# Value products of dilated local attention: the first halving as an accumulating DMA, longer VectorE steps, and h scaled when it is made

## The chip, the cores and the metric

The kernel runs on one NeuronCore of a Trainium2 chip. The metric is the device time of one execution in microseconds; less is better. The chip's engines run side by side, each in the order of its own instructions: TensorE (PE in the profile) does matrix products into eight PSUM banks, VectorE (DVE) does elementwise work on two operands, ScalarE (ACT) does copies and activations, GpSimd (POOL) here issues DMAs, and SyncE (SP) issues DMAs too.

## The reference

All inputs are bf16. `x` is 2048 x 1024.

```python
qkv = x @ wqkv                                   # 32 heads of 32; W, dil = 8, 2
idx = pos[:, None] - off[None, :]                # off = 0, 2, .. 14; masked where < 0
logits = einsum("bhsd,bhswd->bhsw", q, kg) * Dh ** -0.5     # kg = k[idx]
attn = softmax(where(mask, logits, -1e9))
a = einsum("bhsw,bhswd->bhsd", attn, vg) @ wo    # vg = v[idx]
b = (gelu(x @ w_gate) * (x @ w_up)) @ w_down     # Df = 3584
g = sigmoid((x * gate_w).sum(-1, keepdims=True))
return g * a + (1 - g) * b
```

So every position attends to itself and seven earlier positions at distances 2 to 14, in each head; a gated MLP runs beside it; a scalar gate per position mixes the two.

## The kernel before

**The products.** All large products go through a seven-product scheme (Strassen in Winograd's form): sums and differences of the blocks of both operands are made by VectorE, seven block products by TensorE, and their results are combined in PSUM by ScalarE's copies and VectorE's additions. The sequence is cut in two halves `s` of 1024 positions (`SUP`), these into chunks of 512 (`SC`). A `Unit` is one such product of the first stage: 28 matmuls of 128 x 512. There are 78 of them, in a written order: gate and up of pair 1 for half 0, 16 for q and k, 8 for v, then gate and up for the other pairs of hidden columns. There are `NPAIR` = 14 pairs; `NE_` = 12. In unit `b` TensorE runs p1 of `b`, p73 of `b - 1`, p5 and p26 of `b`, p4 of `b - 1`. Behind p73 stands VectorE's evacuation (L403), which reads the banks of two products that p4 and later steps write again.

**Background work.** All else on VectorE is done in tasks, Python generators that emit one step and yield its cost. At the end of each unit `run_bg` (L442) adds a period (4.7 before unit 26, then 4.8, and more where logit reductions take TensorE time) to a credit, keeping at most 0.3 of what was left, and takes steps of the first task in order of priority until the credit is at 0.3 or below. A step that yields None puts its task off to the next unit. So the order of VectorE's instructions is fixed when the kernel is written out, and depends on the costs that the tasks state.

- `h_task` (priority 0): `h_store` (L253) multiplies gelu(gate) by up for one pair and half (2048 elements a partition), and stores it to `h_d` by a DMA on GpSimd's queue. For the last two pairs it also multiplies by `omgrep`, which holds 1 - g.
- `sums_pair` (1): sums of the next pair's weights. `softmax` and `softmax_back` (1 and 3): one to three attention blocks of 256 positions (`AC`); the weights, times g, go to `attn_all` and from there to `w_d` in HBM.
- `qk_prods` (2): for one tile `t` of eight and one half, three products q by eight shifted k, 8 x 256 elements each, into `prod` tiles; TensorE sums them over the partitions of a head (`reduce_mm`). `spill` (4): the same for the fourth block of each half, where eight tiles are multiplied and added up on VectorE in two groups of four before the reduction.
- `t_forms`: sums of blocks of `w_down` and `wo`, stored in `t_d`.
- `pv_all` (4.2, then 5; L727): for each of eight blocks, in the order `PVO`, the attention weights come back from `w_d`, repeated over the partitions of a head, into `ab_`, and v from `v_d` into `vb`. For each of eight tiles one multiplication makes 2048 products (8 window positions by 256) in `prod2`, and for two tiles together the window is folded by three additions (L752), of 2048, 1024 and 512 elements:

```python
def mult(t):
    TT(out=prod2[(t // 2) % 2][:, t % 2], in0=ab, in1=_win_ap(v[:, t, HALO:HALO + AC], ...), op=ALU.mult)
def fold(t, w):
    ...
    TT(out=out_, in0=h(0), in1=h(1), op=ALU.add)      # w = 4, 2, 1
```

  A finished block goes from `ob_` to `o_d`.

**The down products.** From 512 us on, `down(0)` and `down(1)` multiply h and the attention output, as one matrix of 18 tiles (`NK`), by `w_down` and `wo`, for each half, in the seven-product scheme, and for most products once more inside (`level2`, matmuls of 128 x 256). Blocks A11 to A22 are loaded from `h_d` and `o_d`; where h was not scaled in `h_store`, `scale_task` (L913) multiplies it by `omgrep` after the load: for half 0 in the last units and at the start of `down(0)`, for half 1 within `down(1)`.

Of the kernel before, what the change touches and what calls it, by code (L numbers as in the profile page):

```python
# [9 lines left out]
ALU = mybir.AluOpType  # L10
# [5 lines left out]
P = 128  # L16
# [6 lines left out]
NJ = 4  # L23
# [45 lines left out]
def kernel(  # L69
# [54 lines left out]
    NE_ = NPAIR - 2  # L124
    h_d = [[tc.dram_tile([P, 4, k, SC], BF16, name=f"h_d{s}{e}") for e, k in enumerate((NE_, NPAIR - NE_))] for s in range(2)]
# [6 lines left out]
    w_d = tc.dram_tile([NBLK, 32, NJ, SC], BF16, name="w_d")  # L132
# [4 lines left out]
    with tc.manual_schedule(engines={mybir.EngineType.PE, mybir.EngineType.DVE, mybir.EngineType.Activation,  # L137
# [115 lines left out]
        def h_store(G, U, i, s):  # L253
            TT(out=flat(G), in0=flat(G), in1=flat(U), op=ALU.mult)  # L254
            if i >= NE_:
                om = omgrep[:, s * SUP:(s + 1) * SUP].rearrange("p (o s) -> p o s", o=1)
                TT(out=G, in0=G, in1=om.to_broadcast([P, 2, SUP]), op=ALU.mult)
            e = int(i >= NE_)
            i0 = 2 * (i - NE_ * e)
            nc.gpsimd.dma_start(out=h_d[s][e][:, :, i0 // 2, :], in_=flat(G).rearrange("p (hc s) -> p hc s", hc=4))  # L260
# [234 lines left out]
        def h_task(G, U, i, s):  # L495
            h_store(G, U, i, s)
            yield 1.14 if i < NE_ else 2.35
# [79 lines left out]
        pr_off = [R_PR + 4 * i for i in range(4)] + [R_PROD + 4 * i for i in range(2)]  # L577
# [3 lines left out]
        ab_ = [reg4(R_AB[i], NJ, NWIN, SJ) for i in range(2)]  # L581
        ob_ = [reg3(R_O[i], NT, AC) for i in range(2)]
        prod2 = [reg4(R_PROD2 + 8 * i, 2, NJ, NWIN * SJ) for i in range(2)]
# [16 lines left out]

        def reduce_mm(lg, src, start, stop):
            for j in range(NJ):
                nc.tensor.matmul(lg[32 * j:32 * j + 32, :], lhsT=R_[:], rhs=src[:, :, j * SJ:(j + 1) * SJ],
                                 start=start, stop=stop)
# [5 lines left out]
        def qk_prods(u, s, t):  # L610
            while reduced[0] < NT * s + t - t % 2:
                yield None
            out_ = []
            for a in range(ND):
                pr = prod_tile()
                qk_mult(pr, u.T[:, 0, a * AC:(a + 1) * AC], u.T[:, 1, a * AC:(a + 1) * AC])
                out_.append(pr)
                yield 1.14
            prods[t] = out_
            if t % 2:  # L620
                slotq.append(lambda: (qk_reduce(s, t - 1, prods[t - 1]), qk_reduce(s, t, out_)))
# [16 lines left out]

        def spill(s):
            while reduced[0] < 2 * NT:  # L640
                yield None
            accs = []
            temps = [prod_tile() for _ in range(2)]

            def mult(t, dst):
                qk_mult(dst, qb[s][:, t, :], kb[s][:, t, HALO:HALO + AC])

            def add(g, t):
                TT(out=accs[g], in0=accs[g], in1=temps[t % 2], op=ALU.add)

            for g in range(NT // QG):
                accs.append(prod_tile())
                mult(QG * g, accs[g])
                yield 1.14
                for t in range(1, QG):
                    mult(QG * g + t, temps[t % 2])
                    yield 1.14
                    if t > 1:
                        add(g, t - 1)
                        yield 1.14  # L660
                add(g, QG - 1)
                yield 1.2
            slotq.append(lambda: spill_reduce(s, accs))
# [36 lines left out]
        def softmax_back(a, cnt, ee, e4, sw, m, bc):  # L700
            while a // BPS not in gated:
                yield None
            d = m
            V.tensor_reduce(out=d, in_=sw, axis=AX.X, op=ALU.add)
            yield 0.9 * cnt + 0.05
            V.reciprocal(out=d, in_=d)
            TT(out=d, in0=d, in1=gblk[:, a:a + cnt, :], op=ALU.mult)
            yield 0.65 * cnt
            TT(out=attn_all[:, a:a + cnt, :].rearrange("p a (w s) -> p a w s", w=NWIN), in0=e4, in1=bc(d), op=ALU.mult)
            yield 0.55 * cnt + 0.05  # L710
            for j in range(NJ):
                nc.gpsimd.dma_start(out=w_d[a:a + cnt, :, j, :].rearrange("a h n -> h a n"),
                                    in_=attn_all[32 * j:32 * j + 32, a:a + cnt, :])
            ready.update(range(a, a + cnt))
            if a == 2 * BPS - 1:
                two[0] = True

        def pv_load(a, i):
            src = w_d[a].rearrange("h j n -> h (j n)")
            nc.sync.dma_start(out=ab_[i % 2].rearrange("p j w s -> p (j w s)"),  # L720
# [6 lines left out]
        def pv_all():  # L727
# [4 lines left out]
            yield None  # L732
            for i, a in enumerate(PVO):
# [8 lines left out]
                v, ab, o_ = vb[i % 2], ab_[i % 2], ob_[i % 2]  # L742

                def mult(t):
                    TT(out=prod2[(t // 2) % 2][:, t % 2], in0=ab,  # L745
                       in1=_win_ap(v[:, t, HALO:HALO + AC], [[SJ, NJ], [-DIL, NWIN], [1, SJ]]), op=ALU.mult)

                def fold(t, w):
                    pr = prod2[(t // 2) % 2]
                    h = lambda k: pr[:, :, :, k * w * SJ:(k + 1) * w * SJ]  # L750
                    out_ = h(0) if w > 1 else o_[:, t:t + 2, :].rearrange("p t (j s) -> p t j s", j=NJ)
                    TT(out=out_, in0=h(0), in1=h(1), op=ALU.add)  # L752

                mult(0)
                yield 1.14
                mult(1)
                yield 1.14
                for t in range(0, NT, 2):
                    if i + 1 == NBLK and t == 2:
                        load_A(Bs(0)["A12"], 0, 1, 0, 0, KX, False)  # L760
                    nxt = t + 2 < NT
                    if nxt:
                        mult(t + 2)
                        yield 1.14
                    fold(t, 4)
                    yield 1.14
                    if nxt:
                        mult(t + 3)
                        yield 1.14
                    fold(t, 2)  # L770
                    yield 0.68
                    fold(t, 1)
                    yield 0.4
                a0 = a % BPS % 2 * AC
                nc.gpsimd.dma_start(out=o_d[a // BPS][a % BPS // 2][:, :, a0:a0 + AC], in_=o_)
# [33 lines left out]
        pv_task = [bg(pv_all(), 4.2, QE + 3)]  # L809

# [53 lines left out]
        def t_forms():  # L864
            for q in range(NQ):
# [7 lines left out]
                for o_, a, b_ in ((r11, r12, r11), (r12, r22, r12), (r22, r22, r11), (r21, r21, r22)):  # L873
                    TT(out=flat(o_), in0=flat(a), in1=flat(b_), op=ALU.subtract)
                    yield 0.71
# [37 lines left out]
        def scale_task(b, s, c, ia, ib):  # L913
            t0 = s * SUP + c * SC
            om = omgrep[:, t0:t0 + SC].rearrange("p (o s) -> p o s", o=1)
            for i0 in range(ia, ib, 4):
# [153 lines left out]
        def down(s):  # L1070
# [112 lines left out]
            if not last:  # L1183
# [3 lines left out]
                take(rest, 3)  # L1187
# [120 lines left out]
```

## Time and profile before

| | |
|---|---|
| median of 3 runs | 720.22 us (719.84 to 720.38) |
| profiled execution | 720.06 us, span of its instructions 718.3 us |
| granted clock of TensorE | 1.000 |
| PE busy | 707.2 us |
| DVE busy | 673.2 us |
| ACT busy | 328.7 us |
| POOL busy | 134.5 us |
| DMA | 162.04 MB, mean 226 GB/s |

The span goes from the first instruction to the last; the execution's time has 1.8 us more around it. Busy time is the time in which an engine has an instruction running; instructions on PE and VectorE overlap a little, so that the sum of the durations is more than the busy time. A group's row has its line in the kernel, engine and operation, out<-in with the shapes, the count, then busy time and mean duration of one, then the engine's idle time just before and what ended it.

### The profile page before, as it was taken

The page shows a single profiled execution, that of the slowest core. Times are in us where ns is not written, and L with a number is a line of the kernel's source. Part 1 is how long each engine was busy: PE and PEld are TensorE (multiplying, and loading weights), DVE is VectorE, ACT ScalarE, POOL GpSimd, SP SyncE. Part 2 cuts the span into 40 slices and gives each one's busy share as a digit, 9 for nine tenths or more (in the row PEclk, how much of TensorE's full clock was granted, in tenths as well). Part 3 has the DMA queues.
Part 4 walks back from the last instruction along what each step waited for, and adds up shares of the span by engine and source line. Part 5 has one row for each costly group of instructions (what it writes and reads, how often), then busy time and mean ns, then how long its engine had stood idle before and what let it go on. Part 6 is the DMA issues. An engine that isn't in the chain of part 4 may idle for free. (4 is left out here: it accounts for less than half of the span.)

```text
span 718.3 us, 10752 instructions
## 1 busy us (share of the span) xinstructions
PE 707.2 (98%) x4051; PEld 408.2 (57%) x4107; DVE 673.2 (94%) x722; ACT 328.7 (46%) x600; POOL 134.5 (19%) x233
## 2 busy tenths in 40 slices
PE   8999999999999999999999999999999999999998
PEld 4466656655544444444444444444447886758887
DVE  2789989999999999999999999999999999899997
ACT  4554546444456665555555555555322321131431
POOL 1323544133210332121300000000210002110011
PEclk9999999999999999999999999999999999999999
DMA  9976643378264758574934836371891899995951
GB/s 276 284 183 219 229 142 122 106 247 304 102 205 127 231 197 252 175 221 149 294 115 152 280 123 214 124 288 59 300 427 52 307 401 396 420 429 223 379 213 60
DMA packets 92276, 162.04 MB, mean 226 GB/s; under 512 B 19280, under 2 KB 68848, under 8 KB 87872
## 3 DMA queue, kind: packets, MB, share of 16 engines
q1 hardware_dynamic: 75520, 105.46, 42.7%
q0 software_dynamic: 15984, 48.29, 19.3%
q10 hardware_dynamic: 720, 7.60, 2.7%
q8 instruction: 32, 0.52, 0.3%
q14 instruction: 20, 0.16, 0.1%
HBM read 112.17 MB, written 54.14 MB: 232 GB/s over the span
## 5 line engine op out<-in xcount | busy, mean ns | idle before, releaser
L366 PE MATMUL banks<-arena 128*128 128x512 bf16 x2136 | 472.1, 379 | 4.2 <-DVE arena L403 0.7
L366 PEld LDWEIGHTS <-arena 128*128 128x128 bf16 x2184 | 240.5, 111 | 235.3 <-issue 7.0
L1046 PE MATMUL banks<-arena 128*128 128x256 bf16 x1260 | 138.9, 273 | 0.8 <-DVE arena L1012 0.6
L1046 PEld LDWEIGHTS <-arena 128*128 128x128 bf16 x1260 | 123.1, 98 | 16.7 <-issue 1.5
L389 ACT COPY arena<-banks 128x512 f32<-128x512 f32 x78 | 45.8, 587 | 130.7 <-PE banks L366 130.7
L403 DVE TENSOR_TENSOR arena<-banks,arena 128x1024 bf16<-128x1024 f32 x78 | 95.2, 1221 | 11.0 <-PE banks L366 5.5
L374 ACT CAST arena<-banks 128x512 bf16<-128x512 f32 x102 | 59.7, 586 | 42.4 <-PE banks L366 42.4
L745 DVE TENSOR_TENSOR arena<-arena 128x2048 bf16<-128x2048 bf16 x64 | 77.0, 1220 | 0.5
L752 DVE TENSOR_TENSOR arena<-arena 128x2048 bf16<-128x2048 bf16 (+2 forms) x96 | 73.9, 776 | 1.0
L598 DVE TENSOR_TENSOR arena<-arena 128x2048 bf16<-128x2048 bf16 x64 | 74.7, 1219 | 0.1
L260 POOL DMA_DIRECT2D h_d<-arena x28 | 20.4, 730 | 226.5 <-DVE arena L254 195.4
L1079 PE MATMUL banks<-arena 128*128 128x512 bf16 x282 | 62.5, 379 | 0.3
L396 ACT COPY banks<-banks 128x512 f32<-128x512 f32 x78 | 44.5, 570 | 21.8 <-PE banks L366 20.0
L1004 DVE TENSOR_TENSOR arena<-arena 128x2304 bf16<-128x2304 bf16 x40 | 53.3, 1352 | 0.5
L384 ACT COPY banks<-banks 128x512 f32<-128x512 f32 x78 | 45.0, 576 | 13.6 <-PE banks L366 12.1
L1051 ACT COPY banks<-banks 128x256 f32<-128x256 f32 x60 | 21.4, 356 | 60.9 <-PE banks L1046 60.7
L1079 PEld LDWEIGHTS <-arena 128*128 128x128 bf16 x288 | 28.2, 98 | 33.5
L927 DVE TENSOR_TENSOR arena<-arena 128x2048 bf16<-128x2048 bf16 (+1 forms) x40 | 41.8, 1111 | 1.3 <-DMA arena<-h_d 1.3
L372 ACT ACTIVATE arena<-banks 128x512 bf16<-128x512 f32 x54 | 32.2, 597 | 15.4 <-PE banks L366 15.3
L323 DVE TENSOR_TENSOR arena<-arena 128x1024 bf16<-128x1024 bf16 x60 | 38.6, 685 | 0.5
L1012 DVE TENSOR_TENSOR arena<-arena 128x2304 bf16<-128x2304 bf16 x28 | 37.7, 1351 | 0.2
L254 DVE TENSOR_TENSOR arena<-arena 128x2048 bf16<-128x2048 bf16 x28 | 34.0, 1216 | 1.9 <-ACT arena L251 1.4
(93 smaller groups left out, 435.8 us busy)
## 6 DMA issues: line engine op xcount, KB each, us to landing
arena<-t_d SPq DMA_DIRECT2D x8, 2304.0 KB, 14.4
h_d<-arena POOLq DMA_DIRECT2D x28, 512.0 KB, 4.3
arena<-w_c SPq DMA_DIRECT2D x12, 1152.0 KB, 14.1
t_d<-arena POOLq DMA_DIRECT2D x36, 256.0 KB, 4.3
arena<-h_d SPq DMA_DIRECT2D x6, 1536.0 KB, 12.7
arena<-in_B_w_gate_dram SPq DMA_DIRECT2D x15, 512.0 KB, 5.7
arena<-in_B_w_up_dram SPq DMA_DIRECT2D x15, 512.0 KB, 5.3
arena<-in_B_w_down_dram SPq DMA_DIRECT2D x28, 256.0 KB, 6.6
```

Source lines behind the costliest of these rows:

```text
L366: self.pe = nc.tensor.matmul(ps, lhsT=self.L[form](kt), rhs=rhs[:, kt, :], start=(start and kt == 0), stop=(kt == HK - 1), skip_group_chec ...
L374: nc.scalar.copy(out=o_, in_=i_)
L384: nc.scalar.copy(out=self.Y, in_=self.X)
L389: nc.scalar.copy(out=self.p5s, in_=self.V)
L396: nc.scalar.copy(out=self.Z, in_=self.Y)
L403: TT(out=self.T[:, :, c2s], in0=pair, in1=self.p5s.rearrange("p (o n) -> p o n", o=1).to_broadcast([P, 2, SC]), op=ALU.add)
L598: TT(out=dst, in0=q.rearrange("p (o s) -> p o s", o=1).to_broadcast([P, NWIN, AC]), in1=_win_ap(k, [[-DIL, NWIN], [1, AC]]), op=ALU.mult)
L745: TT(out=prod2[(t // 2) % 2][:, t % 2], in0=ab, in1=_win_ap(v[:, t, HALO:HALO + AC], [[SJ, NJ], [-DIL, NWIN], [1, SJ]]), op=ALU.mult)
L752: TT(out=out_, in0=h(0), in1=h(1), op=ALU.add)
L1004: TT(out=o_, in0=a, in1=b_, op=op)
L1046: nc.tensor.matmul(c(i, h, j), lhsT=l[:, kt, j * P:(j + 1) * P], rhs=r[:, kt, :], start=False, stop=(kt == KH - 1), skip_group_check=True)
L1079: nc.tensor.matmul(ps, lhsT=L[:, i, j * P:(j + 1) * P], rhs=R[:, i, :], start=(start and q == 0), stop=(q == NK - 1), skip_group_check=not ...
```

## The change

- **Value products.** `mult` makes one tile, or two in one instruction of 4096 elements where the credit is above 1.5. The addition that folds eight window positions to four is no longer done by VectorE: a DMA on GpSimd's queue adds the upper half of the products of two tiles onto the lower half (512 KB onto 512 KB, in SBUF). The two smaller folds stay on VectorE; they are emitted one pair of tiles later and at the earliest in the next unit. `ab_` and `w_d` are laid out by window position and all 256 positions, so `w_d` is written by more and smaller stores.
- **Logits.** `qk_prods` and `spill` join two multiplications, and `spill` two additions, in one instruction where the credit is above 1.5; the `prod` tiles are ordered so that two lie at a fixed distance.
- **T forms.** Two of the four subtractions are joined.
- **h.** `h_store` scales every pair but pairs 0 and 1 of half 0. These two are loaded once more, scaled and stored by a new task, `early_h`. `scale_task` does nothing any more.

```diff
+    EARLY_H = ((0, 0), (1, 0))
-    w_d = tc.dram_tile([NBLK, 32, NJ, SC], BF16, name="w_d")
+    w_d = tc.dram_tile([NBLK, 32, NWIN, AC], BF16, name="w_d")
@@ h_store, h_task
-            if i >= NE_:
+            if (i, s) not in EARLY_H:
                 om = omgrep[:, s * SUP:(s + 1) * SUP].rearrange("p (o s) -> p o s", o=1)
                 TT(out=G, in0=G, in1=om.to_broadcast([P, 2, SUP]), op=ALU.mult)
-            yield 1.14 if i < NE_ else 2.35
+            yield 1.14 if (i, s) in EARLY_H else 2.3
@@ tiles
-        pr_off = [R_PR + 4 * i for i in range(4)] + [R_PROD + 4 * i for i in range(2)]
+        pr_off = [R_PR, R_PR + 4, R_PROD, R_PR + 8, R_PR + 12, R_PROD + 4]
-        prod2 = [reg4(R_PROD2 + 8 * i, 2, NJ, NWIN * SJ) for i in range(2)]
+        prod2 = reg3(R_PROD2, 4, NWIN * AC)
@@ qk_prods (spill alike)
-            for a in range(ND):
-                pr = prod_tile()
-                qk_mult(pr, u.T[:, 0, a * AC:(a + 1) * AC], u.T[:, 1, a * AC:(a + 1) * AC])
-                out_.append(pr)
-                yield 1.14
+            while a < ND:
+                if a == 0 and credit[0] > 1.5:
+                    qk_mult2(pair_at(pr_off[k], pr_off[k + 1]), u.T[:, 0, 0:AC], u.T[:, 1, 0:AC], AC, AC)
+                    a += 2
+                    yield 2.21
+                else:
+                    qk_mult(out_[a], u.T[:, 0, a * AC:(a + 1) * AC], u.T[:, 1, a * AC:(a + 1) * AC])
+                    a += 1
+                    yield 1.14
@@ softmax_back
             for j in range(NJ):
-                nc.gpsimd.dma_start(out=w_d[a:a + cnt, :, j, :].rearrange("a h n -> h a n"),
-                                    in_=attn_all[32 * j:32 * j + 32, a:a + cnt, :])
+                for i in range(a, a + cnt):
+                    nc.gpsimd.dma_start(out=w_d[i][:, :, j * SJ:(j + 1) * SJ],
+                                        in_=attn_all[32 * j:32 * j + 32, i, :].rearrange("h (w s) -> h w s", w=NWIN))
@@ pv_all
+            def mult(i, t, m):
+                TT(out=prod2[:, t % 4:t % 4 + m, :],
+                   in0=flat(ab_[i % 2]).rearrange("p (o n) -> p o n", o=1).to_broadcast([P, m, NWIN * AC]),
+                   in1=_win_ap(vb[i % 2][:, t, HALO:HALO + AC], [[KV, m], [-DIL, NWIN], [1, AC]]), op=ALU.mult)
+            def folds(i, a, t, asked):
+                if now[0] <= asked:
+                    yield None
+                o_ = ob_[i % 2]
+                for w in (2, 1):
+                    h = lambda k: prod2[:, t % 4:t % 4 + 2, k * w * AC:(k + 1) * w * AC]
+                    TT(out=h(0) if w > 1 else o_[:, t:t + 2, :], in0=h(0), in1=h(1), op=ALU.add)
+                    yield 0.61 if w > 1 else 0.35
+                ...
                 for t in range(0, NT, 2):
-                    if i + 1 == NBLK and t == 2:
+                    if i + 1 == NBLK and t == 4:
                         load_A(Bs(0)["A12"], 0, 1, 0, 0, KX, False)
-                    ...
+                    if credit[0] > 1.5:
+                        mult(i, t, 2)
+                        yield 2.21
+                    else:
+                        for u in range(2):
+                            mult(i, t + u, 1)
+                            yield 1.14
+                    pr = prod2[:, t % 4:t % 4 + 2, :]
+                    nc.gpsimd.dma_start(out=pr[:, :, 0:4 * AC], in_=pr[:, :, 4 * AC:8 * AC], accum_op=ALU.add)
+                    behind.append((i, a, t, now[0]))
+                    if len(behind) > 1:
+                        yield from folds(*behind.pop(0))
+            yield from folds(*behind.pop(0))
@@ new task
+        def early_h():
+            t_ = reg4(R_TF[0], 4, 2, SC)
+            nc.sync.dma_start(out=t_, in_=h_d[0][0][:, :, 0:2, :])
+            yield None
+            for c in range(2):
+                v = _win_ap(t_[:, c, 0, 0:1], [[4 * SC, 2], [SC, 2], [1, SC]])
+                om = _win_ap(omgrep[:, c * SC:c * SC + 1], [[0, 2], [0, 2], [1, SC]])
+                TT(out=v, in0=v, in1=om, op=ALU.mult)
+                yield 1.14
+            nc.gpsimd.dma_start(out=h_d[0][0][:, :, 0:2, :], in_=t_)
+        bg(early_h(), 4.5, NQKV + 3)
@@ t_forms
-                for o_, a, b_ in ((r11, r12, r11), (r12, r22, r12), (r22, r22, r11), (r21, r21, r22)):
+                TT(out=both, in0=_win_ap(flat(r12), [[2 * n_, 2], [1, n_]]), in1=both, op=ALU.subtract)
+                yield 1.14
+                for o_, a, b_ in ((r22, r22, r11), (r21, r21, r22)):
                     TT(out=flat(o_), in0=flat(a), in1=flat(b_), op=ALU.subtract)
-                    yield 0.71
+                    yield 0.61
@@ scale_task, down
+            ib = min(ib, 0)
-                take(rest, 3)
+                take(rest, 2)
```

## The prediction

> **What bounds the kernel now.** I read the busy times first, then TensorE's timeline for its gaps, then VectorE's timeline between two gaps, then the groups by shape, then the DMA issues. The first line of the page:
>
> ```profile
> PE 707.2 (98%) x4051; PEld 408.2 (57%) x4107; DVE 673.2 (94%) x722; ACT 328.7 (46%) x600; POOL 134.5 (19%) x233
> ```
>
> TensorE (PE) is idle for 11.1 us of 718.3. Its timeline, asked in pieces, gives the idle before each stretch in brackets. After the start-up (first 20 us) there are seven: 0.43 at 43.37, 0.21 at 78.72, 0.31 at 118.78, and
>
> ```profile
> 175.74 4.48 PE L366 MATMUL banks<-arena 128*128 128x512 bf16 x20 [0.46 <-DVE arena L403]
> 510.16 2.75 PE L366 MATMUL banks<-arena 128*128 128x512 bf16 x12 [0.28 <-DVE arena L403]
> 663.32 49.48 PE L1046 MATMUL banks<-arena 128*128 128x256 bf16 x450 [0.63 <-DVE arena L1012]
> 712.97 2.13 PE L1046 MATMUL banks<-arena 128*128 128x256 bf16 x18 [0.18 <-DVE omgrep L1203]
> ```
>
> They sum to 2.50 us. The rest of the 11.1 is the start, 3.1 us behind the last matmul, and 0.11 us or so in each 20 us where matmul records are missing. The windows show the same pace wherever attention, h or the down products run:
>
> ```profile
> 300.00:320.00 20.00, 19.89 (x93) 9.04 (x94) 19.49 (x23) 11.03 (x18) 5.21 (x8) 1.00 0.59 174
> 460.00:480.00 20.00, 19.89 (x93) 9.08 (x93) 19.82 (x22) 11.79 (x20) 2.29 (x3) 1.00 0.71 249
> ```
>
> The columns are PE, PE's loads, DVE, ACT, POOL, clock, DMA share, GB/s. 92 to 93 matmuls in 20 us is 0.217 us each at clock 1.00, so a unit of 28 lasts 6.07 us. The change leaves the matmuls alone: it can win about 2.5 us at most, and it loses whatever makes TensorE wait.
>
> What would make it wait is VectorE (DVE), in order and nearly full. Its timeline:
>
> ```profile
> 314.00 1.23 DVE L403 TENSOR_TENSOR arena<-banks,arena 128x1024 bf16<-128x1024 f32 x1
> ...
> 317.34 3.49 DVE L745 TENSOR_TENSOR arena<-arena 128x2048 bf16<-128x2048 bf16 x3
> 320.75 1.22 DVE L403 TENSOR_TENSOR arena<-banks,arena 128x1024 bf16<-128x1024 f32 x1
> ```
>
> Instructions of 2048 elements follow each other every 1.14 us (the 1.22 overlap). Each unit has one evacuation (L403, 1.14) and 4.8 us of background steps: 5.94 of 6.07, 0.13 spare. L403 was due 6.07 after 314.00, at 320.07, and started 0.68 late; TensorE shows no gap there. How late it may be: behind the products that L403 reads TensorE has 12 matmuls (2.6 us) before it needs the bank; less 1.22 that is 1.4, with the semaphore 1.3 us. This is the cover of everything below. Once used up, it comes back at only 0.13 us a unit.
>
> **The change part by part.** The rows by shape:
>
> ```profile
> L745 DVE TENSOR_TENSOR arena<-arena 128x2048 bf16<-128x2048 bf16 x64 | 77.0, 1220 | 0.5
> L752 DVE TENSOR_TENSOR arena<-arena 128x2048 bf16<-128x2048 bf16 x32 | 39.0, 1218 | 0.0
> L254 DVE TENSOR_TENSOR arena<-arena 128x2048 bf16<-128x2048 bf16 x28 | 34.0, 1216 | 1.9 <-ACT arena L251 1.4
> L257 DVE TENSOR_TENSOR arena<-arena,omgrep 128x2048 bf16<-128x2048 bf16 x4 | 4.9, 1225 | 0.1
> L918 DVE TENSOR_TENSOR arena<-arena,omgrep 128x2048 bf16<-128x2048 bf16 x23 | 26.8, 1217 | 0.0
> ```
>
> *VectorE's sum.* Out: 32 first halvings (the 2048 form of L752) at 1.14, 36.4. Out: the scaling of h before the down products, 23 at 1.14 and two short ones, 27.4, of which some 14 lay around the end of the units and 14 in the second half's down products. In: L257 grows from 4 to 26, 25.0; two multiplies of `early_h`, 2.3. Joined steps: 1024 elements take 0.60 and 2048 take 1.14, so an instruction costs 0.07 by itself and a joined pair saves that; 16 in the logits, about 7 in the left-over blocks, about 21 of 32 in the values (the rest find under 1.5 of credit and stay single), 9 in the T forms: 3.7. Net -40, VectorE about 633 us busy. None of it is on TensorE's path while the background budget stays 4.8 a unit: it ends the attention earlier (the last o_d store some 30 us sooner), no more.
>
> *What TensorE gets back.* The 0.63 at 663.32 sits in the second half's down products, where 10 us of scaling leave VectorE ahead of it; the 0.28 at 510.16 is the crowded last unit; the 0.18 may go too. -1.1. The gaps before 180 us have other causes; joined steps there overrun the credit as single ones do (up to 0.8): 0, between -0.8 and +0.6.
>
> *Small additions, at nothing.* The w_d stores go from 20 to 32, in pieces of 128 bytes, at 32 KB each, the size that landed in 1.8 us (6.1 at most); values are read a unit or more later. The load of A12 moves one step later in the last block, on SP's queue, some 40 us before its products. Where the scaling of A11 to A22 had waited for their loads, the products now do; the chain of loads is as before or earlier, since attention ends earlier. The extra load of 1 MB on SP's queue (early h) has two units (12 us) to land, by the order of priorities; a 1 MB load took 9.7. If it gets only one unit, VectorE waits 3.6 and TensorE 2.3. Its store and the 32 adding DMAs cost GpSimd 0.73 each, 24 us on an engine busy for 19%; behind them on its queue stand stores of h and o_d and copies to w_c, read many units later.
>
> *The new wait.* Each of 32 steps now issues a DMA that adds 512 KB to 512 KB in SBUF, and the next fold on VectorE waits for it to land; behind that fold on VectorE stands L403, for which TensorE waits. So two times matter: the landing, L, and the time from issue to fold.
>
> The second I get from the credits. In two units there are 9.6: 2.3 for h, 1.28 on average for weight sums, leaving 6.0, and a pair of value tiles costs 2.21+0.61+0.35 = 3.17. So 32 pairs take about 35 units (34 to 70 of 78). Laying steps out unit by unit, the fold behind an issue comes after: the earlier folds (0.95), L403 (1.14, at times with a short wait) and the next pair (2.21), 4.3 us, in 3 of 32 cases; the same with h (2.27) in place of some of it, 5.9 to 6.7, in 8; 8.1 to 8.5 in 3; over 10 in 18.
>
> No row shows an adding DMA. The nearest:
>
> ```profile
> h_d<-arena POOLq DMA_DIRECT2D x28, 512.0 KB, 4.3
> arena<-in_A_wqkv_dram SPq DMA_DIRECT2D x6, 1024.0 KB, 9.7
> o_d<-arena POOLq DMA_DIRECT2D x8, 512.0 KB, 7.1
> k_d<-arena POOLq DMA_DIRECT2D x16, 68.0 KB, 1.9
> ```
>
> Low end: a plain 512 KB store, 4.3. High end: 1 MB, 9.7. From 68 to 512 KB the landing grows by 2.4; the sum moves three blocks (two read, one written) where a store moves two, so 1.9 + 1.5 x 2.4 = 5.5, and with a DMA share of 0.61 that these transfers raise, I take 5.7, nearest to the store of the same size and queue. Spread: of 21 h stores from 250 to 510 us most landed in 3.3 to 5.4, but one in 9.9 while bulk loads ran; I give 1 in 5 adding DMAs 1.4 more (7.1) and 1 in 12 5.3 more (11).
>
> Price, each as L less the time to the fold less 1.3, where above zero. At 5.7: 3 x 0.1 = 0.3; one in five at 7.1, 3 x 0.2 x 1.5 = 0.9; one in twelve at 11, 3/12 x 5.4 + 8/12 x 3.6 + 3/12 x 1.4 = 4.1. Together 5.3, less some overlap, 5.0. At 4.3 only the late ones count, about 2. At 7.1 the three short ones always wait (4.5), the eight find the cover gone about half the time (4), and the tail adds 4: 12.5. At 9.7 VectorE runs behind throughout: 3 x 5.4 + 8 x 3.6 = 45.
>
> The Trainium skill's page "Collectives: The Full Stack", section on the bandwidth ceiling, says that an add in the DMA path reads two sources per write and moves at half a copy's rate, the read side being the limit. By that rule, as an estimate, the moving part doubles: 1.9 + 4.8 = 6.7, and the price would be about 10 instead of 5. No run here shows such a transfer yet.
>
> **Sum.** Profiled execution 720.06 (span 718.3 and 1.8 around it) - 1.1 + 5.0 = 723.96. The median of the runs is 0.16 higher: 724.1, said as 724.0.
>
> **Rivals.**
> - *The wait is hidden.* If the DMAs land within 4.3 and seldom late (18 of 32 have over 10 us), only -1.1 is left: 719.1 to 719.2. For: the folds are put off by a unit; against: three gaps of 4.3 and the 9.9 row.
> - *Faster.* As before, and VectorE's relief also ends the gaps before 180 us: -2.5 in all, 717.7. It decides where steps of the logits and left-over blocks stop overrunning. Against: three of those gaps name ACT, issue and the first weight sums.
> - *The adding DMA is slow.* From L = 8 on, VectorE is late in every pair of units and TensorE keeps its pace: 720 - 1 + 20 at 8, + 45 at 9.7: 739 to 765.
> - *It does less than it says*: with little credit the steps stay single. It is in the sum (21 of 32) and moves only VectorE's idle time.
>
> **How the numbers follow.** A measurement here can tell some 0.2% (1.44 us) from no change. My forecast (some waits, 721 to 737) has 0.46; hidden 0.27; faster 0.12; slow DMA 0.15. Faster: 0.12 and 0.02 from the lower edge of hidden, 0.14. Same: 0.25 from hidden and 0.01 of mine, 0.26. Slower: 0.45 + 0.15 = 0.60. Forecast's own range 721 to 737. For 8 in 10, low 718.2 (leaves out most of faster, 0.08) and high 738 (leaves out 0.10 of slow).
>
> **What would show it.** VectorE busy near 633; L257's group at 26; scaling gone; the last o_d store near 475 instead of 505; adding DMAs landing at 5.7 in the median; idle before the folds named DMA arena<-arena, and TensorE gaps <-DVE L403 between 250 and 465 us, in sum about 5. Wrong if those gaps are under 1 (hidden) or over 18 (slow), or if TensorE waits anew elsewhere: for early h, for weights behind it, or in the down products.

## The result and the profile after

| | before | after |
|---|---|---|
| median of 4 runs | 720.16 us (719.84 to 720.38) | 764.52 us (764.13 to 766.04) |
| ratio, 95% interval | | 1.062 (1.060 to 1.064) |
| span of the profiled execution | 718.3 us | 762.5 us |
| granted clock of TensorE | 1.000 | 0.982 |

The kernel became 44 us slower, outside the predicted range (718.2 to 738.0), on the side that had the larger chance, and within the time given for the rival "the adding DMA is slow" (739 to 765). The first line of the page has VectorE's relief as forecast, and TensorE no longer full:

```profile
PE 722.5 (95%) x4107; PEld 410.6 (54%) x4107; DVE 636.5 (83%) x636; ACT 328.9 (43%) x600; POOL 182.7 (24%) x278
```

The waits view names who waited for whom; its columns are us in total, times, longest us:

```profile
DVE arena L766 <- DMA arena<-arena: 38.5, 11, 6.4
PE banks L367 <- DVE arena L404: 33.3, 13, 6.3
```

L766 is the fold on VectorE behind the adding DMA, L404 the evacuation (L403 before). Before, TensorE waited 0.7 us in sum for the evacuation. VectorE waits for eleven of the 32 adding DMAs, and TensorE then waits for the evacuation that stands behind the fold. The timeline shows the first case whole (start, duration, and the idle time ahead of it in brackets):

```profile
272.17 0.74 POOL L261 DMA_DIRECT2D h_d<-arena  x1 [3.01 <-ACT arena L412]
272.84 0.83 POOL L841 DMA_DIRECT2D h_d<-arena  x1
273.98 1.21 POOL L792 DMA_DIRECT2D arena<-arena  x1 [0.31 <-DVE arena L766]
274.88 2.28 DVE L756 TENSOR_TENSOR arena<-arena 128x4096 bf16<-128x4096 bf16 x1
282.99 1.15 DVE L766 TENSOR_TENSOR arena<-arena 128x1024 bf16<-128x1024 bf16 x2 [5.83 <-DMA arena<-arena]
284.18 2.29 DVE L756 TENSOR_TENSOR arena<-arena 128x4096 bf16<-128x4096 bf16 x1
286.38 1.22 DVE L404 TENSOR_TENSOR arena<-banks,arena 128x1024 bf16<-128x1024 f32 x1
287.65 4.59 PE L367 MATMUL banks<-arena 128*128 128x512 bf16 x11 [5.89 <-DVE arena L404]
```

The products are ready at 272.77, but GpSimd has two stores to `h_d` to issue first (the second, L841, is that of `early_h`) and issues the adding DMA at 273.98. VectorE makes the next pair of products and is ready for the fold at 277.16, only 3.2 us after the issue. The sum lands 9.0 us after its issue, and VectorE, which works in order, stands still for 5.83. The joined product of the pair after that and then L404 come next, and TensorE has idled 5.89. The last line, cut off where the view ends at 292 us, holds a second loss: 11 matmuls in 4.59 us are 0.42 each, half pace. The windows of before and after over the same 20 us (PE, its loads, DVE, ACT, POOL, clock, DMA share, GB/s) have it as a clock:

```profile
280.00:300.00 20.00, 19.95 (x94) 9.05 (x93) 19.66 (x24) 11.62 (x19) 5.79 (x8) 1.00 0.66 220
```

and after:

```profile
280.00:300.00 20.00, 14.11 (x57) 5.83 (x55) 15.55 (x18) 6.77 (x11) 4.64 (x6) 0.83 0.94 231
```

57 matmuls instead of 94. The clock is 0.83 and the DMA share 0.94 instead of 0.66. The issues have the adding DMA at 8.4 us, and show that some of what shares the 16 DMA engines lands later too (KB each, median us to landing):

```profile
arena<-arena POOLq DMA_DIRECT2D x32, 512.0 KB, 8.4
h_d<-arena POOLq DMA_DIRECT2D x28, 512.0 KB, 4.6
arena<-in_B_w_up_dram SPq DMA_DIRECT2D x15, 512.0 KB, 9.6
```

The up weights took 5.3 before and take 9.6; the stores of h moved only from 4.3 to 4.6.

The sum of the loss, from the two profiles: 33.3 - 0.7 = 32.6 us more idle behind evacuations. The clock: one less the granted clock, times 10 us, over the 10 us behind each of the six gaps of 3 us and more (0.79, 0.83, 0.83, 0.85, 0.85 and 0.83), about 10. (The same sum over whole windows gives 14, but part of the slowed time lies within the gaps, where there is no matmul to slow down.) The gaps of 0.63 and 0.18 in the down products are gone, -0.8. These make about 42 against a span that grew by 44.2; some 2 stay unassigned.

### The profile page after: what moved, and what is told of

Same layout as the page of the kernel before. It is cut to its first block, busy times and chain, and to the rows that moved or that the text cites. A ratio compares the mean times of both kernels' runs of the same rounds, so it can differ in the third digit from the quotient of the medians.

```text
span 762.5 us, 10785 instructions
## 1 busy us (share of the span) xinstructions
PE 722.5 (95%) x4107; PEld 410.6 (54%) x4107; DVE 636.5 (83%) x636; ACT 328.9 (43%) x600; POOL 182.7 (24%) x278
## 4 chain that ended last, share of the span: by engine, by line
PE 68%; DMA 13%; DVE 8%; SPq 6%; issue 4%; POOL 1%; ACT 1%; POOLq 0%; DVEq 0%; ACTq 0%
PE banks L367 40%; PE banks L1085 18%; DMA arena<-arena 10%; PE banks L1118 8%; SPq L341 4%; DVE arena L404 3%; PE banks L611 2%; DMA arena<-in_B_w_up_dram 2%; DVE arena L766 1%; DVE arena L756 1%; DMA h_d<-arena 1%; SPq L168 1%; DVE arena L255 1%; SPq L337 1%; DVE arena L258 1%
## 5 line engine op out<-in xcount | busy, mean ns | idle before, releaser
L367 PE MATMUL banks<-arena 128*128 128x512 bf16 x2184 | 487.1, 385 | 34.4 <-DVE arena L404 33.3
L404 DVE TENSOR_TENSOR arena<-banks,arena 128x1024 bf16<-128x1024 f32 x78 | 95.1, 1220 | 29.6 <-PE banks L367 26.1
L756 DVE TENSOR_TENSOR arena<-arena 128x2048 bf16<-128x2048 bf16 (+1 forms) x43 | 74.9, 1743 | 0.8
L766 DVE TENSOR_TENSOR arena<-arena 128x1024 bf16<-128x1024 bf16 x64 | 35.6, 556 | 39.5 <-DMA arena<-arena 38.5
L1118 PE MATMUL banks<-arena 128*128 128x512 bf16 x288 | 62.8, 379 | 0.0
L792 POOL DMA_DIRECT2D arena<-arena x32 | 39.2, 1225 | 61.8 <-DVE arena L756 60.8
L606 DVE TENSOR_TENSOR arena<-arena 128x4096 bf16<-128x4096 bf16 x20 | 45.6, 2284 | 0.3
L966 DVE TENSOR_TENSOR arena<-arena 128x2048 bf16<-128x2048 bf16 (+1 forms) x40 | 41.8, 1115 | 3.3 <-DMA arena<-h_d 3.3
L255 DVE TENSOR_TENSOR arena<-arena 128x2048 bf16<-128x2048 bf16 x28 | 34.1, 1217 | 7.8 <-ACT arena L375 6.4
## 6 DMA issues: line engine op xcount, KB each, us to landing
arena<-h_d SPq DMA_DIRECT2D x6, 1536.0 KB, 12.6
```

The lines of the kernel that those rows point to most:

```text
L367: self.pe = nc.tensor.matmul(ps, lhsT=self.L[form](kt), rhs=rhs[:, kt, :], start=(start and kt == 0), stop=(kt == HK - 1), skip_group_chec ...
L404: TT(out=self.T[:, :, c2s], in0=pair, in1=self.p5s.rearrange("p (o n) -> p o n", o=1).to_broadcast([P, 2, SC]), op=ALU.add)
L606: TT(out=dst, in0=_win_ap(q, [[sq, 2], [0, NWIN], [1, AC]]), in1=_win_ap(k, [[sk, 2], [-DIL, NWIN], [1, AC]]), op=ALU.mult)
L756: TT(out=prod2[:, t % 4:t % 4 + m, :], in0=flat(ab_[i % 2]).rearrange("p (o n) -> p o n", o=1).to_broadcast([P, m, NWIN * AC]), in1=_win_a ...
L766: TT(out=h(0) if w > 1 else o_[:, t:t + 2, :], in0=h(0), in1=h(1), op=ALU.add)
L1118: nc.tensor.matmul(ps, lhsT=L[:, i, j * P:(j + 1) * P], rhs=R[:, i, :], start=(start and q == 0), stop=(q == NK - 1), skip_group_check=not ...
```

## The experiments

Two theories. *Distance*: what counts is the time from an adding DMA's issue to its fold against the time that it takes to land; given more of it, the same bytes cost nothing. *Traffic* (the rival): 32 transfers of 512 KB beside the loads crowd the DMA engines, so that weights and values come late wherever the fold stands. Besides, the other parts of the change (longer steps, buffers laid out anew, h scaled when made) might cost or gain by themselves.

**The DMA by itself.** A kernel with DMAs only: copies and adding DMAs of 512 and 256 KB within SBUF, first beside a stream of loads from HBM, then on an idle chip. It leaves out the whole computation.

> Not the kernel: GpSimd-queue DMAs by themselves, one after the other, four of each form (512 KB plain copy, 512 KB adding, 256 KB plain, 256 KB adding, all within SBUF in runs of 2 KB; 512 KB adding in runs of 4 KB; 512 KB store to HBM), first on an idle chip, then three of each beside a stream of large loads. Theory A (an adding DMA moves twice what a copy moves): alone 512 KB adding lands in about 5.2 us, the least seen in the changed kernel, plain in 3.0 to 3.5, and 256 KB adding in 3.5; beside loads 512 KB adding takes 8 or more. Rival B (the landing is long because the DMA waits in its queue behind others, not by itself): adding and plain land alike, 3.0 to 3.5 alone.

The DMA issues of four stretches, in this order: plain copies beside the loads, adding DMAs beside the loads, plain ones idle, adding ones idle:

```profile
rows<-rows POOLq DMA_DIRECT2D x5, 512.0 KB, 8.9
...
rows<-rows POOLq DMA_DIRECT2D x4, 512.0 KB, 11.7
...
rows<-rows POOLq DMA_DIRECT2D x3, 512.0 KB, 3.1
...
rows<-rows POOLq DMA_DIRECT2D x3, 512.0 KB, 5.0
```

The first line counts five because its stretch also holds the start of the first adding DMA (12.0 us); the four copies took 9.0, 7.6, 8.9 and 7.7, in the middle 8.3. With 256 KB it is 2.3 plain and 3.3 adding on the idle chip. So the adding costs 1.9 us over a copy on an idle chip and 3.4 us beside loads, but the loads themselves cost more, 5.2 for a copy and 6.7 for an adding DMA. This is as the first expectation had it, not the second. These halves lie in two runs of 2 KB a partition, as in the changed kernel; with one run of 4 KB an adding DMA of 512 KB took 4.6 idle and 9.0 beside the loads. The 8.4 of the changed kernel lies between the idle 5.0 and the 11.7 of DMA engines that are always busy.

**Only the addition away.** The DMAs stay, as plain copies.

```diff
-nc.gpsimd.dma_start(out=pr[:, :, 0:4 * AC], in_=pr[:, :, 4 * AC:8 * AC], accum_op=ALU.add)
+nc.gpsimd.dma_start(out=pr[:, :, 0:4 * AC], in_=pr[:, :, 4 * AC:8 * AC])
```

> The changed kernel with the adding left out: each of the 32 DMAs copies the upper half over the lower half instead of adding it, same bytes written, same queue, same places (so the attention sums are not formed). Theory A (reading a second operand makes the landing long): the landing's median falls from 8.4 to about 5, VectorE's waits before the folds from 38.5 us to under 8, time 720 to 727. Rival B (any 512 KB DMA here lands late, for the queue and the other transfers): landing stays at 7.5 to 8.5, time 755 to 765.

741.09 us, ratio 1.029 (1.026 to 1.031), between the two expectations. The copies land in 6.1 in the median:

```profile
DVE arena L766 <- DMA arena<-arena: 17.8, 7, 4.3
PE banks L367 <- DVE arena L404: 17.5, 12, 4.4
```

2.3 us less of landing halve the loss (21.0 of 44 are left). The loss depends steeply on the landing time, as the prediction's list of prices had it; this run doesn't tell distance from traffic, since a plain copy also reads half as much.

**Parts alone.** Two kernels: the first halving back on VectorE with h scaled as before, which leaves the longer steps and the new layouts; and the adding DMA alone, with no steps joined and h scaled as before (the load of A12 is put off to where the attention then is). The joined subtractions of the T forms stay in both.

```diff
 # the longer steps and layouts alone
-nc.gpsimd.dma_start(..., accum_op=ALU.add)
-for w in (2, 1):
+for w in (4, 2, 1):
 # the adding DMA alone
-if credit[0] > 1.5:          # each of the four places that join steps
+if credit[0] > 99:
 # both
-if (i, s) not in EARLY_H:
+if i >= NE_:
```

> The changed kernel with the first halving back on VectorE and h scaled after the load as before: the longer steps and the new layouts alone. Theory: nothing waits on a DMA, VectorE's budget per unit is as before, so 719 to 721. Rival D (the longer steps overrun the background budget and delay the evacuations): 722 or more, with gaps behind the evacuation before 250 us.

> The adding DMA alone: the changed kernel with steps in q k, left-over blocks and values kept single, and h scaled after the load as before (A12 loaded no earlier than 12 units from the end). Theory A (the adding DMA carries the loss): attention runs ahead faster, so more folds are close behind their DMA, and the time is 755 to 775. Rival E (the loss needs the h scaling or the longer steps in front of the fold): under 740.

The steps and layouts alone: 726.23, ratio 1.009 (1.007 to 1.012). The adding DMA alone: 777.18, ratio 1.079 (1.078 to 1.080), with

```profile
DVE arena L766 <- DMA arena<-arena: 52.4, 15, 7.9
```

So the adding DMA carries the whole loss, and the rest of the change lessens it by 13: there 15 folds wait, here 11. That fits the distances, since more other work on VectorE between issue and fold (scaling h of all pairs) puts the fold off; the two parts were not parted further. That the longer steps and layouts alone lose 6 was not forecast, and the expectation's rival has the time but not the place: their long gap lies at 513 us, not before 250. Whether the joined steps do it:

> Edit, against the kernel with the first halving back on VectorE and h scaled pair by pair as before (726.2 us): no step of VectorE is joined with the next any more, all else is that kernel's. If the joined steps cost the 6 us there: 720 to 722, the matmuls' idle time back to 2.5 to 3.5 us in sum. If the moved buffers and the order of the folds cost them: 725 to 727, with the idle time at 5 us or more.

728.82 (725.99 to 730.24), ratio 1.010 (1.009 to 1.012). Single steps are no better, so the loss lies in what is left, the layouts and the order of folds above all, and not in the joining of products and folds. Both kernels have several short gaps behind evacuations and one long one, here that of the kernel without joins:

```profile
517.69 4.44 PE L367 MATMUL banks<-arena 128*128 128x512 bf16 x12 [2.29 <-DVE arena L404]
```

Which layout or which move in the order costs them was not settled.

**The copies to w_c earlier.** The 21 copies to `w_c` run beside the attention, and the twelve of them with 384 KB from `w_down` land in 8.6 instead of 6.3; here all stand at units 4 to 21, ahead of it.

```diff
-at(NQKV + 10 + 6 * m_ + e_, lambda k_=k_, i_=i_: lay_out(k_, i_))
+at(4 + 6 * m_ + e_, lambda k_=k_, i_=i_: lay_out(k_, i_))
```

> The changed kernel with only the copies to w_c (21 DMAs, 7 MB read and written) moved from units 36 to 53 to units 4 to 21. Theory A with shared DMA engines (landing 8.4 is 5.0 alone plus sharing with other transfers): landing of the first 16 adding DMAs falls from about 8.7 to 6.5, fold waits before 400 us from 16 to under 8 us, time 745 to 757. Rival B' (the landing is set by the adding DMA itself): landing 8 or more, time 760 to 767.

760.86, ratio 1.057 (1.054 to 1.059): 10 folds wait 33.2 us, landing 7.6. Less traffic beside the attention gives 4 us of 44. The time is the one that the rival had, the landing lies between the two.

**Folds two pairs behind.** A third slot of products, and the fold emitted two pairs after its DMA.

```diff
-prod2 = reg3(R_PROD2, 4, NWIN * AC)
+prod2 = [reg3(o, 2, NWIN * AC) for o in (R_PROD2, R_PROD2 + 8, R_PROD)]
-if len(behind) > 1:
+if len(behind) > 2:
```

> The changed kernel with a third slot for the products of two tiles, so that the folds come two pairs behind the DMA instead of one. Theory A (the whole loss is landing 8.4 against a time to the fold of 3 to 7 us in a third of the cases): the time to the fold rises to 10 us or more in nearly all of 32 cases, waits fall under 6 us, granted clock back to 1.00, time 719 to 724. Rival C (the adding DMAs slow the weight loads and stores, and these hold the kernel up): the DMA traffic is the same, so the time stays above 740.

757.87, ratio 1.052 (1.051 to 1.053), though the fold waits fell from 38.5 to 7.1:

```profile
DVE arena L324 <- DMA arena<-in_B_w_up_dram: 25.2, 4, 13.1
DVE arena L769 <- DMA arena<-arena: 7.1, 2, 4.0
PE banks L367 <- DVE arena L404: 31.2, 12, 12.2
SPq L855 <- DMA o_d<-arena: 38.5, 1, 38.5
```

The loss only changed its name: VectorE now waits for up weights. It looked like the rival. But the last line shows SP's queue held for 38.5 us by one load (of A12), which waits for a store to `o_d`, that is for the end of an attention block; the weights' loads stand behind it. The load of R11 reaches into the new slot's place and waits too (8.0 us). Two tries to move these: the slot at 83 KB and A12's load behind the last fold; then also the w_c copies early and a unit's period of 4.5 (in this last kernel the third slot's late products overwrite part of A11).

```diff
-... for o in (R_PROD2, R_PROD2 + 8, R_PROD)]
+... for o in (R_PROD2, R_PROD2 + 8, 83)]
-if i + 1 == NBLK and t == 4:
-    load_A(Bs(0)["A12"], 0, 1, 0, 0, KX, False)     # now behind the last fold
 # the second of the two also
-run_bg(b, (4.7 if b < NQKV else 4.8) + extra)
+run_bg(b, 4.5 + extra)
```

> The third slot again, but clear of the memory of the R11 load and with the load of A12 behind the last fold, so that SP's queue is not held by either. In the first third-slot run the waits for adding DMAs fell from 38.5 to 7.1 us, and waits of the weight sums for weights (25.2) took their place. Theory A (both come from the place of these transfers in the queues): weight waits under 4 us, fold waits under 7, time 721 to 728. Rival C (the adding DMAs' traffic itself makes the weights late): weight waits stay near 25 and the time above 745.

> As x_d2b, with the copies to w_c issued in units 4 to 21, where DMAs are idle for over half of the time, and VectorE's background period at 4.5 in all units (attention then ends near unit 75 of 78). Theory A: landing near 6 to 7 instead of 8.4, fold waits and overrun gaps nearly gone, time 718.3 to 721. Rival D (shifting w_c or the shorter period makes something else late, such as q and k or the last blocks): 722 or more.

742.88, ratio 1.032 (1.029 to 1.034), and 749.67, ratio 1.040 (1.036 to 1.043); neither comes near its first expectation. Only the trace of the second is read here. In it the folds wait no more than 0.8 us, yet:

```profile
DVE arena L324 <- DMA arena<-in_B_w_up_dram: 18.2, 4, 8.2
PE banks L367 <- DVE arena L404: 22.5, 5, 7.3
```

The timeline of SP's queue around one of these:

```profile
325.95 0.55 SPq L740 DMA_DIRECT2D arena<-w_d  x1
326.68 0.56 SPq L743 DMA_DIRECT2D arena<-v_d  x1
327.33 0.86 SPq L168 DMA_DIRECT2D arena<-in_B_w_gate_dram  x1
328.29 4.62 SPq L168 DMA_DIRECT2D arena<-in_B_w_up_dram  x1
```

The request for the next block's attention weights (L740) has waited 20.9 us for its buffer, until VectorE had made the last products that read it, and has held the request for v and the MLP's weights behind it on SP; then 2 MB are requested within 2.5 us, and the up weights land 16.8 us after issue. (The changed kernel has such waits too, 99.0 us in sum against 93.3 here, so the longer distance is not what makes them.) Late weights by a held queue or by too many bytes (traffic)? The next kernel moves requests and no bytes.

**Two pairs behind, and SP's queue free.** The slot at 100 KB, R11's and A12's loads at the end of the attention, a block's v requested at the second pair of the block ahead of it (`t == 2`; the expectation calls it the third), w_c early, period 4.6.

```diff
+if t == 2 and i + 1 < NBLK:
+    pv_load(PVO[i + 1], i + 1)        # was: at the start of block i
+load_R(Bs(0)["R11"], 0, 0)            # behind the last fold, with A12
```

> Edit, against the changed kernel: the folds run two pairs behind the adding DMA (three product slots, the third at 100 KB), the loads of A12 and R11 go to the end of the attention, the request for a block's v goes out at the block's third pair so that SP's queue isn't held by it, the down weights are copied at units 4 to 21, and the unit's period is 4.6 in the plan. The same bytes move. Theory A (the loss is the distance between an adding DMA and its fold, and what the two earlier tries with more distance still lost was SP's queue being held, which made up-weights late): VectorE waits under 4 us in sum for the folds and under 4 us in sum for the weights, the matmuls' idle time behind evacuations falls from 33.3 us to under 7, time 720 to 727. Rival C (the bytes themselves, 32 adding DMAs beside the loads, make transfers late wherever the issues stand): the weights' waits stay over 12 us in sum with landings of up-weights over 12 us, time over 736.

731.49 us, ratio 1.015 (1.013 to 1.016): it falls between the two expectations, but the profile parts them. The adding DMAs still land in 7.9 in the median, and the DMA share is 0.77 to 1.07 in each 20 us from 280 to 480, yet TensorE hardly waits there and the weights cost VectorE 0.9 us, where the rival had over 12. Only the folds wait longer than the first expectation allowed (12.6 instead of under 4):

```profile
DVE arena L324 <- DMA arena<-in_B_w_up_dram: 0.9, 1, 0.9
DVE arena L769 <- DMA arena<-arena: 12.6, 3, 6.4
PE banks L367 <- DVE arena L404: 8.5, 6, 4.0
```

What is left is in one place, the windows from 460 to 520:

```profile
460.00:480.00 20.00, 20.00 (x94) 9.11 (x93) 19.66 (x18) 11.02 (x18) 6.04 (x6) 1.00 0.88 206
480.00:500.00 20.00, 15.98 (x62) 6.52 (x60) 9.44 (x13) 6.72 (x12) 1.93 (x2) 0.83 1.03 351
500.00:520.00 20.00, 17.66 (x75) 7.60 (x74) 7.78 (x8) 9.23 (x16) 1.60 (x2) 0.91 0.82 275
```

There the last three adding DMAs run beside the bulk loads of h and w_c (1.2 to 1.5 MB each) and land after 7.9, 16.9 and 20.9 us. VectorE is idle half of the time and could have made those sums itself.

**The last pairs back on VectorE.** Three of 32 first halvings (the last pairs of the last block), or the eight of the last two blocks:

```diff
+if i == NBLK - 1 and t >= 2:          # the other kernel: i >= NBLK - 2
+    TT(out=pr[:, :, 0:4 * AC], in0=pr[:, :, 0:4 * AC], in1=pr[:, :, 4 * AC:8 * AC], op=ALU.add)
+else:
     nc.gpsimd.dma_start(..., accum_op=ALU.add)
```

> Edit, against the kernel with folds two pairs behind and the requests moved (731.5 us there): the last three pairs of the last block of eight have their first halving on VectorE (1.14 us each, 3.4 in all), 29 of 32 keep the adding DMA. In that kernel the matmuls hardly idle before 480 us; what it still loses is 4.0 + 2.3 us of gaps and a clock of 0.83 and 0.91 at 480 to 520 us, behind three fold waits of 12.6 us in sum, whose adding DMAs landed beside 3 MB of h and 2.2 MB of weights. Theory A (the loss is where an adding DMA lands too late for its fold, and only there): those waits go, 719.5 to 723. Rival (the end of the attention is late for another cause, VectorE's own work there or the reads of h): the gap stays above 3 us, 727 to 732.

> The same edit for all eight pairs of the last two blocks (of eight) (9.1 us of VectorE more than with the adding DMA): 24 of 32 pairs keep the adding DMA. Theory A: 719.5 to 724, like the kernel with the last three, or up to 2 us above it where VectorE runs late by the 5.7 us more that it is given in 430 to 480 us. Rival (what else stands at the end of the attention): 727 to 732.

| | time | ratio, 95% |
|---|---|---|
| last three | 721.90 us (719.15 to 722.83) | 1.0008 (0.9996 to 1.0020) |
| last eight | 721.97 us (720.03 to 724.22) | 1.0013 (1.0002 to 1.0024) |

Both fall where "distance" had them. With the last three on VectorE, 29 adding DMAs run, and:

```profile
arena<-arena POOLq DMA_DIRECT2D x29, 512.0 KB, 7.6
```

```profile
DVE arena L769 <- DMA arena<-arena: 0.8, 2, 0.6
PE banks L367 <- DVE arena L404: 1.5, 4, 0.5
```

The DMAs are nearly as slow as in the changed kernel, 7.6 instead of 8.4 us, the DMA share from 255 to 500 us is 0.87, and they cost nothing that can be measured. The traffic as such is ruled out as the cause; it costs time through a landing that is longer than the distance, and through weights that come late where a held queue bunches their requests. This kernel differs from the changed one in several things at once (the distance, SP's order, the copies to `w_c`, the period, three halvings); the waits in the profile tell what each was for, but no run has the distance by itself with SP's queue free. The kernel is no faster than before either: TensorE was full before, and is full again.

## Why the prediction was wrong

**The bound, and the gains: right.** TensorE sets the time and VectorE's order makes it wait. VectorE busy was forecast at 633 and is 636.5; the products got 21 of 32 pairs joined, as said. L258 (L257 before) has the 26 multiplies:

```profile
L258 DVE TENSOR_TENSOR arena<-arena,omgrep 128x2048 bf16<-128x2048 bf16 x26 | 31.9, 1225 | 0.9
```

The gaps of 0.63 and 0.18 in the down products went. The load for early h cost nothing. Of the relief nothing could be gained beyond that 1 us; the best kernel of the experiments, no faster than before, agrees.

**The distances: right from the products, too long from the issue.** Forecast for 32 folds: 3 at 4.3 us from the issue, 8 at 5.9 to 6.7, 3 at 8.1 to 8.5, 18 over 10. Read off the timeline after (issue to the moment when VectorE is ready for the fold): 5 from 3.2 to 4.1, 7 from 5.1 to 6.7, 4 from 7.0 to 8.0, 5 from 9.0 to 9.8, 11 from 10.3 up. Counted from the end of the products it is 5 at 4.4, 5 from 5.4 to 7.0, 3 from 7.9 to 8.3, 3 from 9.3 to 9.9 and 16 over 10, near to the forecast: VectorE's steps were laid out rightly, and the five short ones have the forecast's folds, evacuation and pair between. The prediction took the issue to come with the end of the products; it comes 0.3 us later in most cases and up to 5.0.

**The landing: the step that failed.** The term was L = 5.7 with a price of 5.0. It measured 8.4, and by the prediction's own prices (20 at 8, 45 at 9.7) that is about 26; 33.3 was measured. The bytes were not the mistake: on an idle chip the DMA lands in 5.0, and 5.5 was worked out from three blocks moved instead of two. The step took the landing from stores that ran at a DMA share of 0.57 and allowed 0.2 us for the transfers' own load on the engines. From 255 us on until the last folds the share was 0.57 before and 0.90 after, and at such a share the transfer waits among others: 8.3 plain and 11.7 adding where it is always full. Even the tail (7.1, for one in five) lies below the measured median. And the tail was read too short: of the h stores between 250 and 510 us before, four landed after more than 5.4 us (6.0, 7.7, 8.8 and 9.9), where the prediction names one.

The Trainium skill's "Collectives: The Full Stack", section on the bandwidth ceiling, has an add read two sources per write at half a copy's rate. The runs agree for the moving part: from 256 to 512 KB a copy takes 0.8 us more (2.3 to 3.1) and an adding DMA 1.7 (3.3 to 5.0). The 6.7 worked out from it is nearer to 8.4 than 5.7, but not for the reason that made the landing long: on the idle chip 6.7 is too much (5.0), and sharing is not in it.

**The cover, once used up: half seen.** The excess of each fold wait over the cover of 1.3 sums to 25.4 over the nine that exceed it; the other 8 us I put down to waits that met a cover already gone, which the prediction had only from L = 7.1 on.

**The clock: missing.** The price counted idle time alone. Gaps longer than 3 us also lowered the clock behind them, about 10 us in all, near a quarter of the loss.

**GpSimd's part: mis-sized, and seen only from one side.** An adding DMA costs 1.21 us to issue in the median instead of 0.73 for a store. The prediction asked what stands behind the adding DMAs on GpSimd's queue, not what stands ahead of them. Three of the 32 stand behind a store of h that waits for ScalarE, and go out 4.7 to 5.0 us after their products. In one of these the fold waits for it; its products were ready at 427.62:

```profile
431.70 0.75 POOL L261 DMA_DIRECT2D h_d<-arena  x1 [5.21 <-ACT arena L373]
432.37 1.32 POOL L792 DMA_DIRECT2D arena<-arena  x1
441.78 1.15 DVE L766 TENSOR_TENSOR arena<-arena 128x1024 bf16<-128x1024 bf16 x2 [2.91 <-DMA arena<-arena]
```

Issued at once and landing as slowly (9.4 us), it would have been there in time. With 0.9 us of the case at 273.98, some 3.8 of the 38.5 us of fold waits come from GpSimd's order, as an estimate.

**The joined steps at nothing, and the last o_d store near 475: wrong.** The steps and layouts alone lose 6 us (not by the joins; by which of the rest was not settled). The last o_d store was issued at 522.7, later than before (505.2). The stalls are a part of it; in the best kernel, which has none, it still came at 494.7.

**The rivals.** "The adding DMA is slow" happened, with the time and at the place given for it, and had only 0.15: its condition, L from 8 on, was judged by the median of stores in a kernel without the 32 transfers. That even its upper edge fits is in part luck: at the measured 8.4 it gives about 745 (720 - 1 + 26), and the rest is the clock, which it did not have, and the cover that did not come back. "Hidden" comes near with the order of the experiments' best kernel, where the distances exceed the landing: 721.90 against 720.65 for the kernel before in the same runs, so no loss clear of noise, but not the gain of 1.1 either.

## What to carry to other kernels

Work that is moved from an in-order engine to a DMA isn't free because the engine is relieved: compare the landing time, at the DMA share that the change itself brings about, with the shortest time from issue to the first use, one by one, and see what stands ahead of the issue on its queue. Where it is longer, put the use further behind and look at once at what shares the queues, since a longer distance puts off the stores that later loads wait for, and a load that waits holds every load behind it (38.5 us here). A stall of some 3 us on TensorE should be priced with the slower clock behind it.

## What the runs showed of the hardware

- **The clock after a gap.** Of the 41 gaps of 1.5 us and more on TensorE between 230 and 540 us in nine kernels, none of the 9 below 2.0 us, 2 of the 6 from 2.1 to 2.8 (2.29 us did in one kernel and not in another) and 25 of the 26 of 3.05 and more (all but one of 3.36) were followed by a stretch at half clock. From 2.7 to 5.7 us of the stretch lay behind the gap, which costs 1.3 to 2.9 us. In each of the eight traces that have them these stretches last 3.41 us or a multiple of it, and start at whole multiples of 3.41 us from one another (in the changed kernel 17, 26, 42, 51 and 70 behind the first). The Trainium skill's "TensorE: Matmul & The Clock Gate", section "What's actually happening", says that the gate looks at a free-running window of about 3.4 us. The traces agree, and the same gap with two outcomes fits such a window; that 2.3 us can be enough is less than a whole one.
- **Adding within SBUF.** 512 KB onto 512 KB, in runs of 2 KB, lands after 5.0 us on an idle chip and 11.7 beside a full stream of loads (copies: 3.1 and 8.3); in runs of 4 KB after 4.6 and 9.0.
- **Its issue.** GpSimd takes 1.2 us to issue an adding DMA of 512 KB and 0.72 for a plain copy of the same size, both within SBUF in runs of 2 KB (the kernel with DMAs only).
